# T5-bias attention and a squared-ReLU layer on one core: scores of two key tiles in one run over four banks, last queries and keys as block diagonals, six-token rows, weights in blocks

## The chip, the cores and the metric

The kernel runs on one core of a Trainium2 chip. The metric is the device time of one execution in microseconds. Inputs and output are float32; inside the kernel the operands of the matrix products are float16.

## The reference

Eight batches of eight heads, 576 tokens, head size 64. A bias that depends on the distance of query and key alone, through a table of 32 buckets, is added to the scores; the attention's output, laid out as 4608 tokens by 512, goes through two dense layers with a squared ReLU between them.

```python
scores = scale * np.matmul(q, k.transpose(0, 1, 3, 2))      # scale = 1/8
bias = bias_table[bucket]                                   # bucket of abs(i - j), 32 of them
scores = scores + bias.transpose(2, 0, 1)[None, :, :, :]
attn = softmax(scores)
x = np.matmul(attn, v)  -> (4608, 512)
h = np.maximum(x @ w_in, 0.0)                               # w_in 512 x 2048
return h * h @ w_out                                        # w_out 2048 x 512
```

## The kernel before

The work is cut into 32 head pairs (four in each batch) and nine groups of 512 tokens for the dense layers.

**A head pair** (`pair`, L492). The q and k of two heads lie in a staging tile with 128 tokens on the partitions. Five transposes on PE for each of q and k (L504) turn them into `qt` and `kt`: 128 partitions, of which 64 belong to each head, by 576 tokens. The copy out of PSUM (`copy_to`, L478) goes to ACT or DVE. Scores are computed transposed, keys on the partitions. For each of the four full key tiles (`jt` 0 to 3) and each half of the queries (288) there is one step of two matmuls (L528): each uses 64 of the 128 rows of the array, one head each, and each writes a PSUM bank of its own. The 64 tokens that are left over as keys (`jt` 4) are done by four matmuls on quarters of the array (L535). ACT takes the exponential of each step's 2 x 288 columns (L554). DVE multiplies the stretches near the diagonal by the exponentials of the bias (L574); farther off the bias is constant and drops out. PV (L612 and L619) is done for three and then two query tiles: nine matmuls for each tile, which also give the sums of the softmax; DVE divides (L636, L641). After four pairs the batch's output `x` is transposed on PE (L663) and copied to `xt`.

**A group of the dense layers** (`layers`, L693): 16 pieces of the first layer, four matmuls of 512 columns each (L758), ReLU on ACT (L778) and the square on DVE (L786); then 16 pieces of the second layer, four matmuls each (L707), a scaled copy (L727, L733) and a store.

**PSUM** has eight banks: two sets of two for scores (`st`), one for PV (`pv`), three (`f`) for transposes and the dense layers.

**What sets the order.** Nothing is issued in the order of the code. `Plan` collects every step with its engine, a guess of its cost, what it depends on, what buffers it takes and a due time. `schedule` (L88) then runs a list schedule on these guesses and the instructions are emitted in the order of their planned starts. On the chip each engine runs its list in that order and waits where it must. When PE changes between modes (`"r"` for the matmuls on 64 rows, `"q"` for the quarters, `"f"` for all others) the plan adds `SWITCH`, 60 ns. The due time of pair `p` is `nominal(p)`.

**Loads.** All of q, k, v and the weights go through POOL's queue (L243), which casts them to float16. In batch 0 q and k come by head pair: two DMAs of 128 tokens by 4 by 64 and one of 64 tokens for each (L372); in later batches by token tile, all heads at once (L395). The weights `w_in` come in four blocks of 128 rows (L436), and the first matmul of the first layer needs all four; the second layer needs all of `w_out` and all 16 squares. The bias table is built on the chip at the start and goes through DRAM once (`tdram`, L293).

Of the kernel before, what the change touches and what calls it, by code (L numbers as in the profile page):

```python
# [27 lines left out]
XR = 2560  # L28
# [43 lines left out]
LAT = {"PE": 200.0, "ACT": 90.0, "DVE": 90.0, "POOL": 120.0, "DMA": 0.0, "SP": 0.0}  # L72
SWITCH = 60.0


class Plan:
# [11 lines left out]
    def schedule(self):  # L88
        engines = ("PE", "ACT", "DVE", "POOL", "SP", "DMA")
# [57 lines left out]
    @staticmethod  # L147
    def _buf_time(op):
        t = 0.0
        for b in op.bufs:  # L150
            if b.slot is None:
                if not b.ring.free:
                    return float("inf")
                t = max(t, min(b.ring.free)[0])
        return t
# [15 lines left out]
def kernel(  # L171
# [37 lines left out]
    tr_sb = sb("tr_sb", [128, H, 384])  # L209
    tv_sb = sb("tv_sb", [H, 512])  # L210
    oh_sb = sb("oh_sb", [32, 512])
    NSTG, NQK, NPT, NV, NX, NGB, NRT, NY = 2, 5, 2, 3, 2, 2, 4, 3
    stg = [[sb(f"{n}s{i}", [128, 5, 512]) for n in "qk"] for i in range(NSTG)]
    qts = [sb(f"qt{i}", [128, S]) for i in range(NQK)]
    kts = [sb(f"kt{i}", [128, S]) for i in range(NQK)]
# [5 lines left out]
    xs = [sb(f"x{i}", [128, 5, 512]) for i in range(NX)]  # L221
    xt_sb = sb("xt", [128, 4, XR])
    gs = [sb(f"g{i}", [128, 16, GT]) for i in range(NGB)]
    rts = [sb(f"rt{i}", [128, GT]) for i in range(NRT)]
# [14 lines left out]
    def loader(eng_name, eng, out_, in_, packets, deps=(), bufs=(), due=0.0):  # L239

        issue = P.add(
            {eng_name: 800.0 if eng_name == "POOL" else 60.0},
            lambda: io(eng.dma_start(out=out_(), in_=in_())),  # L243
            deps,
            bufs,
            due,
        )
        return P.add({"DMA": packets * 27.0 / 16}, None, [issue], bufs, due), issue
# [4 lines left out]
    def load(eng_name, eng, out_, in_, packets, deps=(), bufs=(), due=0.0):  # L253
# [12 lines left out]
    l_bt = load("SP", nc.sync, const(bt_sb), const(bias_table), 32, due=0)  # L266
    l_far = load(
        "SP", nc.sync, const(far_sb), const(bias_table[NBK - 1 : NBK, :].to_broadcast([NBK, H])), 32, due=1
    )
    l_oh = load("SP", nc.sync, const(oh_sb), const(oh_d.ap()), 32, due=2)  # L270
    l_id = load("SP", nc.sync, const(id_sb), const(id_d.ap()), 128, due=3)
# [21 lines left out]
    o = load("SP", nc.sync, lambda: tdram.ap(), const(tv_sb), 64, [o])  # L293
    o = P.add({"SP": 2000.0}, None, [o])
# [6 lines left out]
            256,  # L301
# [31 lines left out]
    first = []  # L333
    for i in range(NSTG):
        for w in range(2):
            first.append(
                P.add({"DVE": 320.0}, lambda i=i, w=w: io(nc.vector.memset(stg[i][w][64:128, 4, :].bitcast(FP32), 0.0)), due=10 + i)
            )
    for i in range(NPT):
        first.append(P.add({"DVE": 90.0}, lambda i=i: io(nc.vector.memset(pts[i][:, PW:], 1.0)), due=20))  # L340
        first.append(P.add({"DVE": 90.0}, lambda i=i: io(nc.vector.memset(p4s[i][:, S:], 1.0)), due=20))
# [30 lines left out]
    def load_pair(b, w, hp):  # L372
        src = (q, k)[w]
        t = lambda: stg[b_stg[b].slot][w]
        ls = []
        for h in (2 * hp, 2 * hp + 1):
            ls.append(
                load(
                    "POOL", nc.gpsimd,
                    lambda h=h: t()[:, 0:4, ts(h, D)],  # L380
                    const(src[b, h, 0:512, :].rearrange("(t p) d -> p t d", p=128)),
                    512, first[0:4], [b_stg[b]], pdue(),
                )
            )
        ls.append(
            load(
                "POOL", nc.gpsimd,
                lambda: t()[0:64, 4, ds(128 * hp, 128)].rearrange("p (h d) -> p h d", d=D),
                const(src[b, 2 * hp : 2 * hp + 2, 512:576, :].transpose([1, 0, 2])),
                128, first[0:4], [b_stg[b]], pdue(),  # L390
            )
        )
        l_qk[b, w, hp] = ls

    def load_qk(b, w):  # L395
        src = (q, k)[w]
        t = lambda: stg[b_stg[b].slot][w]
        ls = []
        for tt in range(5):
            n = 128 if tt < 4 else 64  # L400
            ls.append(
                load(
                    "POOL", nc.gpsimd,
                    lambda tt=tt, n=n: t()[0:n, tt, :].rearrange("p (h d) -> p h d", d=D),
                    const(src[b, :, ds(128 * tt, n), :].transpose([1, 0, 2])),
                    8 * n, first[0:4], [b_stg[b]], pdue(),
                )
            )
        for hp in range(4):
            l_qk[b, w, hp] = ls  # L410

    def load_v(b):
        ls = []
        for tt in range(4):
            ls.append(
                load(
                    "POOL", nc.gpsimd,
                    lambda tt=tt: vas[b_v[b].slot][:, tt, :, 0:64],
                    const(v[b, :, ts(tt, 128), :].transpose([1, 0, 2])),
                    1024, v_fix[0] + v_fix[1] + v_fix[2], [b_v[b]], pdue(),  # L420
                )
            )
        for e in range(2):
            ls.append(
                load(
                    "POOL", nc.gpsimd,
                    lambda e=e: v4s[b_v[b].slot][ds(64 * e, 64), :, e, 0:64],
                    const(v[b, e::2, 512:576, :].transpose([1, 0, 2])),
                    256, v_fix[0] + v_fix[1] + v_fix[2], [b_v[b]], pdue(),
                )  # L430
            )
        l_v[b] = ls

    l_win, l_wout = [], []

    def load_w_in(kk):  # L436
        l_win.append(
            load("POOL", nc.gpsimd, const(w_in_sb[:, kk, :]), const(moe_w_in[ts(kk, 128), :]), 800, (), (), pdue())
        )

    def load_w_out(u):
# [5 lines left out]
                900, (), (), pdue(),  # L447
# [3 lines left out]
    for hp in range(4):  # L451
        for w in range(2):
            load_pair(0, w, hp)
        if hp == 1:
            load_v(0)
    for w in range(2):
        load_qk(1, w)
    for kk in range(4):
        load_w_in(kk)
    load_v(1)  # L460
    for u in range(4):
# [8 lines left out]
    PERIOD, LEAD, FAST = 10300.0, 12000.0, 5900.0  # L470

    def nominal(p):
        return LEAD + FAST * min(p, 5) + PERIOD * max(p - 5, 0)

    xt_ready = {}
    x_bufs = {}
# [15 lines left out]
    def pair(p):  # L492
        b, hp = divmod(p, 4)
        T = nominal(p)
        after = max(0.0, T - 9000.0)
        qb = Buf(r_qk)
        evac = []
        for w, dst in ((0, qts), (1, kts)):
            bank = Buf(r_g)

            def tr(w=w, bank=bank):
                ps = g_ps[bank.slot].bitcast(FP16)
                for t in range(5):
                    io(nc.tensor.transpose(ps[:, ts(t, 128)], stg[b_stg[b].slot][w][:, t, ts(hp, 128)], id_sb))  # L504

            o = P.add({"PE": 5 * mm(128)}, tr, l_qk[b, w, hp] + [l_id], [bank, b_stg[b]], T - 3000, after, "f")
            evac.append(
                copy_to(
                    S,
                    lambda dst=dst: dst[qb.slot],  # L510
                    lambda bank=bank: g_ps[bank.slot].bitcast(FP16)[:, 0:S],
                    [o], [bank, qb], T - 3000,
                )
            )
        pb = Buf(r_pt)
        exps = {}
        for jt in (4, 0, 1, 2, 3):
            for half in range(2) if jt < 4 else (0,):
                st = Buf(r_set)

                def score(jt=jt, half=half, st=st):
                    kt, qt, ps = kts[qb.slot], qts[qb.slot], sets_ps[st.slot]
                    for hh in range(2) if jt == 4 else (half,):
                        for e in range(2):
                            rows = ds(64 * e, 64)
                            if jt < 4:
                                io(
                                    nc.tensor.matmul(  # L528
                                        ps[:, e, 0:HQ], kt[rows, ts(jt, 128)], qt[rows, ts(hh, HQ)],
                                        start=True, stop=True,  # L530
                                    )
                                )
                            else:
                                io(
                                    nc.tensor.matmul(  # L535
                                        ps[rows, hh, 0:HQ], kt[rows, 512:576], qt[rows, ts(hh, HQ)],
                                        start=True, stop=True,
                                    )
                                )

                o = P.add(
                    {"PE": mm(HQ) + 10 if jt < 4 else 2 * mm(HQ) + 10},
                    score, evac, [st, qb], T, after, "r" if jt < 4 else "q",
                )

                def ex(jt=jt, half=half, st=st):
                    if jt < 4:
# [297 lines left out]
```

## Time and profile before

| | |
|---|---|
| median of three runs | 442.41 us (440.94 to 442.55) |
| the profiled execution's own time | 443.17 us |
| its span, from the first to the last instruction | 441.4 us |
| granted clock, mean over the span | 0.996 |
| ACT busy | 288.0 us (65%) |
| DVE busy | 210.2 us (48%) |
| POOL busy | 119.5 us (27%), all of it issuing loads |

Times in the profile are in us from the start of the span, durations of single instructions in ns. PE is the matrix engine and PEld its weight loads. Matmuls are pipelined: a matmul's duration is longer than the step from its start to the start of the next, so the steps between starts show what it costs. A group's row gives count, busy time, mean duration and, behind the second bar, the idle time ahead of it with what ended it.

### The profile page before, as it was taken

To read this page: it belongs to the slowest core of one execution; us is meant where nothing else is said; L and a number is where in the kernel's file an instruction comes from. 1 tells how busy PE (TensorE), PEld (TensorE's weight loads), DVE (VectorE), ACT (ScalarE), POOL (GpSimd) and SP (SyncE) were. 2 spreads that over 40 slices of the span, in tenths; PEclk is the share of its full clock that TensorE was granted. 3 is DMA by queue.
4 is the path that set the end of the run, shared out by engine and by line. 5 is a ranking of instruction groups with operands and counts; after the bars stand their busy time and mean duration, and the time that the engine had idled before them with its cause. 6 is when DMAs were issued, how large, how long until landed. Compare 5 with 4: busy or idle time off the path is not lost.

```text
span 441.4 us, 9092 instructions
## 1 busy us (share of the span) xinstructions
PE 417.2 (95%) x3713; PEld 209.7 (48%) x3713; DVE 210.2 (48%) x513; ACT 288.0 (65%) x495; POOL 119.5 (27%) x154
## 2 busy tenths in 40 slices
PE   1687999999999999999999999999999999999996
PEld 0265545554455445544454445544454454544442
DVE  3545556445555655455455446465544553352210
ACT  1657787667866876777767666685777766464421
POOL 7998569422162205230254007000000000000000
PEclk9998999999999999999999999999999999999999
DMA  9999999918091808980099009400010001000111
GB/s 131 159 87 165 190 166 122 137 29 76 2 133 28 74 1 74 108 55 24 26 133 79 1 25 113 68 1 25 25 50 1 25 24 49 25 25 25 48 49 72
DMA packets 122170, 29.24 MB, mean 66 GB/s; under 512 B 113896, under 2 KB 117008, under 8 KB 122128
## 3 DMA queue, kind: packets, MB, share of 16 engines
q0 software_dynamic: 115552, 18.36, 56.5%
q1 hardware_dynamic: 6576, 10.30, 6.7%
q8 instruction: 29, 0.48, 0.5%
q14 instruction: 13, 0.11, 0.1%
HBM read 37.55 MB, written 9.45 MB: 106 GB/s over the span
## 4 chain that ended last, share of the span: by engine, by line
PE 91%; DMA 3%; ACT 3%; DVE 2%; issue 1%; SPq 0%; ACTq 0%; DVEq 0%
PE f L707 30%; PE f L758 29%; PE st L528 11%; PE pv L619 9%; PE f L504 4%; PE pv L612 3%; PE st L535 3%; PE f L663 2%; ACT pt L554 2%; DMA tr_sb<-t_bias 1%; DMA t_bias<-tv_sb 1%; DMA oh_sb<-c_oh 1%; SPq L243 0%; DVE pt L574 0%; ACT y L727 0%
## 5 line engine op out<-in xcount | busy, mean ns | idle before, releaser
L554 ACT ACTIVATE pt<-st 128x576 f16<-128x576 f32 x256 | 157.3, 649 | 42.1 <-PE st L528 40.1
L707 PE MATMUL f<-w_out_sb,g 128*128 128x512 f16 x576 | 144.9, 380 | 0.4 <-ACT qt L483 0.3
L758 PE MATMUL f<-xt,w_in_sb 128*128 128x512 f16 x576 | 141.0, 380 | 0.9 <-DVE xt L485 0.4
L778 ACT ACTIVATE rt<-f 128x512 f16<-128x512 f32 x144 | 86.1, 598 | 57.1 <-PE f L758 53.2
L786 DVE TENSOR_TENSOR g<-rt 128x512 f16<-128x512 f16 x144 | 61.1, 425 | 100.6 <-ACT rt L778 100.4
L758 PEld LDWEIGHTS <-w_in_sb 128*128 128x128 f16 x576 | 51.0, 97 | 61.3 <-issue 3.8
L574 DVE TENSOR_TENSOR pt<-pt,tb_sb 128x512 f16<-128x512 f16 (+2 forms) x96 | 59.7, 623 | 40.7 <-ACT pt L554 37.7
L707 PEld LDWEIGHTS <-g 128*128 128x128 f16 x576 | 48.7, 98 | 60.8 <-issue 13.2
L528 PE MATMUL st<-qt,kt 64*128 64x288 f16 x512 | 66.2, 298 | 4.8 <-ACT pt L554 3.7
L243 POOL DMA_DIRECT2D qs<-in_q_dram x47 | 38.1, 834 | 101.4 <-PE f L504 98.1
L619 PE MATMUL pv<-va,pt 128*128 128x65 f16 x1280 | 57.2, 196 | 0.2 <-DVE pt L574 0.2
L619 PEld LDWEIGHTS <-pt 128*128 128x128 f16 x1280 | 52.6, 100 | 5.1 <-issue 0.7
L528 PEld LDWEIGHTS <-kt 64*128 64x128 f16 x512 | 20.2, 94 | 57.8 <-issue 52.9
L243 POOL DMA_DIRECT2D va<-in_v_dram x32 | 28.4, 916 | 43.0 <-PE pv L619 26.9
L243 POOL DMA_DIRECT2D ks<-in_k_dram x47 | 38.2, 858 | 6.3 <-DMA w_out_sb<-in_moe_w_out_dram 3.5
L612 PE MATMUL pv<-vm,pm 128*128 128x130 f16 x160 | 36.1, 225 | 0.2 <-DVE x L641 0.2
L641 DVE TENSOR_TENSOR x<-pv,r 128x384 f16<-128x384 f32 x64 | 31.4, 491 | 2.2
L554 ACT ACTIVATE pm<-st 128x576 f16<-128x576 f32 x32 | 20.8, 651 | 13.0 <-PE st L535 13.0
L636 DVE RECIPROCAL r<-pv 128x6 f32<-128x6 f32 x64 | 11.9, 187 | 26.0 <-PE pv L619 25.7
L727 ACT ACTIVATE y<-f 128x512 f32<-128x512 f32 x20 | 12.0, 598 | 18.6 <-PE f L707 18.2
L504 PE MATMUL f<-id_sb,qs 128*128 128x128 f16 x160 | 15.5, 234 | 4.3 <-DMA qs<-in_q_dram 4.3
L612 PEld LDWEIGHTS <-pm 128*128 128x128 f16 x160 | 15.9, 99 | 6.5 <-issue 1.4
(37 smaller groups left out, 175.7 us busy)
## 6 DMA issues: line engine op xcount, KB each, us to landing
out_dram<-y SPq DMA_DIRECT2D x36, 256.0 KB, 2.0
va<-in_v_dram POOLq DMA_DIRECT2D x32, 128.0 KB, 5.2
qs<-in_q_dram POOLq DMA_DIRECT2D x28, 128.0 KB, 4.6
ks<-in_k_dram POOLq DMA_DIRECT2D x28, 128.0 KB, 5.1
w_in_sb<-in_moe_w_in_dram POOLq DMA_DIRECT2D x4, 512.0 KB, 7.4
w_out_sb<-in_moe_w_out_dram POOLq DMA_DIRECT2D x4, 512.0 KB, 9.5
qs<-in_q_dram POOLq DMA_DIRECT2D x15, 64.0 KB, 4.8
ks<-in_k_dram POOLq DMA_DIRECT2D x15, 64.0 KB, 4.7
```

The source lines that it names most:

```text
L243: lambda: io(eng.dma_start(out=out_(), in_=in_())),
L504: io(nc.tensor.transpose(ps[:, ts(t, 128)], stg[b_stg[b].slot][w][:, t, ts(hp, 128)], id_sb))
L528: nc.tensor.matmul(ps[:, e, 0:HQ], kt[rows, ts(jt, 128)], qt[rows, ts(hh, HQ)], start=True, stop=True,)
L554: nc.scalar.activation(out=dst, in_=sets_ps[st.slot][:, :, 0:HQ], func=EXPF, scale=SCALE)
L574: io(nc.vector.tensor_tensor(out=a, in0=a, in1=t, op=MULT))
L612: nc.tensor.matmul(ps[:, i, :, :], pm[:, c : c + 128], vm[:, hp, :, 0:65], start=True, stop=False)
L619: nc.tensor.matmul(ps[:, i, e, :], pt[:, (2 * jt + e) * S + c : (2 * jt + e) * S + c + 128], va[:, jt, 2 * hp + e, 0:65], start=False, sto ...
L641: nc.vector.tensor_tensor(out=xs[xb.slot][:, qt0 : qt0 + nq, ts(hp, 128)].rearrange("p t (e d) -> p t e d", e=2), in0=ps[:, :, :, 0:64], i ...
L707: nc.tensor.matmul(g_ps[bank.slot], gs[gb.slot][:, nt, ts(m, 128)], w_out_sb[:, nt, :], start=(nt == 0), stop=(nt == 15),)
L758: nc.tensor.matmul(g_ps[bank.slot], w_in_sb[:, kk, ts(nt, 128)], xt_sb[:, kk, c : c + GT], start=(kk == 0), stop=(kk == 3),)
L778: nc.scalar.activation(out=rts[rb.slot], in_=g_ps[bank.slot], func=RELUF)
L786: nc.vector.tensor_tensor(out=gs[gb1.slot][:, nt, :], in0=rts[rb.slot], in1=rts[rb.slot], op=MULT)
```

## The change

1. **Scores in full banks.** For each key tile and head there is now one matmul of 512 queries that fills a bank (L604), and from batch 1 on two key tiles form one step of four matmuls over both sets: `run([0, 1])`, `run([2, 3])`. In batch 0 the key tiles are done singly. One exponential covers 2 x 512 columns. A step of two key tiles needs both sets free when it starts.
2. **Last queries and last keys as block diagonals.** Four small copies in each pair (L586), on DVE or on POOL as the plan finds, spread the last 64 columns of `qt` and `kt` over two 64 by 64 blocks on the diagonal of tiles `qz` and `kz` that are otherwise zero. With them the last 64 queries of both heads take four matmuls of 128 columns on the full array (L628), and the last 64 keys two of 288 columns (L653); each of the two has one exponential.
3. **Six-token rows.** In batches 0 and 1 a partition of the staging tile holds six tokens in a row, so that q and k are read in runs of 1536 bytes (384 float32) on 96 partitions in place of runs of 256 bytes. Their transposes (L559) are twelve, of 96 rows, with 64 output columns each, the two heads side by side; the copy out of PSUM puts the tokens back in order. From batch 2 on q and k are loaded by head, and the staging tile is laid out by head pair.
4. **Weights in blocks.** `w_in` comes in four blocks of 512 columns, and a piece of the first layer waits for its own block only; a quarter of the second layer waits for its own block of `w_out` and its own four squares. The order of the loads puts q, k and v of batch 0 first.
5. **The plan.** `SWITCH` is 105 ns; DMA costs are in ns for each packet; the due times come earlier (`LEAD` 8000 for 12000, `FAST` 4500 for 5900, `PERIOD` 9500 for 10300); PV is put at 300 ns a query tile in place of 508. The ring `xt` is four batches long (2304 columns), so group 4 takes its columns in two pieces. `tr_sb` lies in a buffer of the dense layers.

The functions for a transpose by DMA (`DT_QK`, `DT_X`) are not used with the values given. The diff, cut to what the steps above speak of:

```diff
-LAT = {"PE": 200.0, "ACT": 90.0, "DVE": 90.0, "POOL": 120.0, "DMA": 0.0, "SP": 0.0}
-SWITCH = 60.0
+LAT = {"PE": 200.0, "ACT": 90.0, "DVE": 90.0, "POOL": 120.0, "DMA": 1800.0, "SP": 0.0, "XB": 2000.0}
+SWITCH = 105.0
...
+    def load_six(b, w, h0, nh):
+        src = (q, k)[w]
+        l = load(
+            "POOL", nc.gpsimd,
+            lambda: six(stg[b_stg[b].slot][w])[:, h0 : h0 + nh, :],
+            const(src[b, h0 : h0 + nh].rearrange("h (p j) d -> p h (j d)", j=6)),
+            96 * nh * 107, (), [b_stg[b]], pdue(),
+        )
...
     for hp in range(4):
         for w in range(2):
-            load_pair(0, w, hp)
+            load_six(0, w, 2 * hp, 2)
         if hp == 1:
-            load_v(0)
+            load_v_tail(0, range(4))
+            for h in range(4):
+                load_v_head(0, h)
+    for h in range(4, 8):
+        load_v_head(0, h)
+    for u in range(4):
+        load_w_in(u)
...
+                if b < SIX:
+                    for j in range(6):
+                        for e in range(2):
+                            io(
+                                nc.tensor.transpose(
+                                    ps[ds(64 * e, 64), ts(j, 96)], six(t)[:, 2 * hp + e, ts(j, D)],
+                                    id_sb[0:96, 0:96],
+                                )
+                            )
...
+                spread.append(one_of({"DVE": 130.0, "POOL": 300.0}, sp, [evac[w]] + z_fix, [qb], T - 1000))
...
+        def run(jts):
+            sets = [Buf(r_set) for _ in jts]
+
+            def score():
+                kt, qt = kts[qb.slot], qts[qb.slot]
+                for jt, st in zip(jts, sets):
+                    for e in range(2):
+                        rw = ds(64 * e, 64)
+                        io(
+                            nc.tensor.matmul(
+                                sets_ps[st.slot][:, e, :], kt[rw, ts(jt, 128)], qt[rw, 0:512],
+                                start=True, stop=True,
+                            )
+                        )
+
+            o = P.add({"PE": len(jts) * mm(512) + 10}, score, evac, sets + [qb, pb], T, after, "r")
...
+        if b < 1:
+            run([0])
+            run([1])
+            last_keys()
+            run([2])
+            run([3])
+        else:
+            run([0, 1])
+            last_keys()
+            run([2, 3])
+        last_queries()
...
-                            {"PE": 4 * mm(512)}, f2, d + squares[g - 1] + l_wout, [bank, gb], 1e6, 0.0, "f"
+                            {"PE": 4 * mm(512)}, f2, d + squares[g - 1][4 * part : 4 * part + 4] + [l_wout[part]], [bank, gb], 1e6, 0.0, "f"
...
-                    {"PE": 4 * mm(512)}, f1, xt_ready[g] + l_win, [bank], due + i * 2000, 0.0, "f"
+                    {"PE": 4 * mm(512)}, f1, xt_ready[g] + [l_win[nt // 4]], [bank], due + i * 2000, 0.0, "f"
```

How the steps stand on the engines. PE's list in the middle of the program before: one step of scores (`st`, line 528) between pieces of the first layer (line 758); `kt` is the keys of a pair, `f` a bank of the dense layers, and the numbers behind the names tell buffers apart.

```order
L758 MATMUL f0_113<-xt_98,w_in_sb_62 128x512
L528 LDWEIGHTS kt2_83
L528 MATMUL st0_110<-qt2_78,kt2_83 128x288
L528 LDWEIGHTS kt2_83
L528 MATMUL st0_110<-qt2_78,kt2_83 128x288
L758 LDWEIGHTS w_in_sb_62
L758 MATMUL f1_114<-xt_98,w_in_sb_62 128x512
```

The same place of PE's list now, in a pair of batch 1: a step of two key tiles, behind the first layer (line 897) and ahead of the transposes of batch 2 (line 566).

```order
L897 MATMUL f1_119<-xt_103,w_in_sb_62 128x512
L604 LDWEIGHTS kt1_80
L604 MATMUL st0_115<-qt1_76,kt1_80 128x512
L604 LDWEIGHTS kt1_80
L604 MATMUL st0_115<-qt1_76,kt1_80 128x512
L604 LDWEIGHTS kt1_80
L604 MATMUL st1_116<-qt1_76,kt1_80 128x512
L604 LDWEIGHTS kt1_80
L604 MATMUL st1_116<-qt1_76,kt1_80 128x512
L566 LDWEIGHTS qs0_71
```

Two pairs of matmuls on half rows now stand together and fill both sets, where one pair stood alone. Counted over PE's whole list, PE leaves the full array for part of it and comes back 182 times before and 69 times now (10 and 11 of these ahead of the first matmul of the dense layers); changes from one kind of part to another, without the full array between, number 17 and 5.

POOL's list of loads at the start, before: `qs` and `ks` are the staging tiles of q and k, `va` and `vm` those of v.

```order
L243 DMA w_in_sb<-in_moe_w_in_dram 128x2048 x2
L243 DMA qs_72<-in_q_dram 128x4x64 x2
L243 DMA qs_72<-in_q_dram 64x2x64
L243 DMA ks_73<-in_k_dram 128x4x64 x2
L243 DMA ks_73<-in_k_dram 64x2x64
```

POOL's list at the start now, up to the first loads of v.

```order
L250 DMA qs_71<-in_q_dram 96x2x384
L250 DMA ks_72<-in_k_dram 96x2x384
L250 DMA qs_71<-in_q_dram 96x2x384
L250 DMA ks_72<-in_k_dram 96x2x384
L250 DMA qs_71<-in_q_dram 96x2x384
L250 DMA vm_98<-in_v_dram 64x4x64 x2
L250 DMA va_95<-in_v_dram 128x4x64 x4
```

Two loads of `w_in` stood ahead of the first q; now the first q is the first load, and one load brings a pair's q where three did. Up to the last block of `w_out` POOL issued 54 loads and now issues 36.

POOL's list now at the loads of batch 4, with the small copies (line 586) that fell to POOL.

```order
L586 COPY qz3_86<-qt3_78 64x64 x2
L250 DMA qs0_71<-in_q_dram 64x4x64 x2
L250 DMA qs0_71<-in_q_dram 128x4x64 x8
L250 DMA ks0_72<-in_k_dram 64x4x64 x2
L250 DMA ks0_72<-in_k_dram 128x4x64 x8
L586 COPY kz0_87<-kt0_79 64x64 x2
```

POOL had only loads before. Now 35 of the 128 small copies stand in its list (the other 93 in DVE's), and some of them stand behind a block of 20 loads.

More of the change, by code (lines that the diff above doesn't have):

```diff
@@ L88, in schedule @@
     def schedule(self):
-        engines = ("PE", "ACT", "DVE", "POOL", "SP", "DMA")
+        engines = ("PE", "ACT", "DVE", "POOL", "SP", "DMA", "XB")
         now = dict.fromkeys(engines, 0.0)
@@ L412, in load_v @@
[L412 to L432, printed above, removed]
@@ L502, in tr @@
                 ps = g_ps[bank.slot].bitcast(FP16)
[L503 to L514, printed above, removed]
+                t = stg[b_stg[b].slot][w]
@@ L516, in pair @@
         exps = {}
[L517 to L547, printed above, removed]
-                        dst = pts[pb.slot][:, 0:PW].rearrange("p (j e s) -> p j e s", j=4, e=2)[
-                            :, jt, :, ts(half, HQ)
-                        ]
-                    else:
-                        dst = p4s[pb.slot][:, 0:S].rearrange("p (h s) -> p h s", h=2)
@@ new lines, in last_keys, with score, ex @@
+        def last_keys():
+            st = Buf(r_set)
+            def score():
+                for half in range(2):
+                    io(
+                        nc.tensor.matmul(
+                            sets_ps[st.slot][:, half, 0:HQ], kzs[qb.slot], qts[qb.slot][:, ts(half, HQ)],
+                            start=True, stop=True,
+                        )
+                    )
+            o = P.add({"PE": 2 * mm(HQ)}, score, evac + spread[2:4], [st, qb, pb], T, after, "f")
+            def ex():
+                io(
+                    nc.scalar.activation(
+                        out=p4s[pb.slot][:, 0:S].rearrange("p (h s) -> p h s", h=2),
+                        in_=sets_ps[st.slot][:, :, 0:HQ], func=EXPF, scale=SCALE,
+                    )
+                )
+            exps["k"] = P.add({"ACT": act(S)}, ex, [o], [st, pb], T)
```

300 lines of the change are left out of this document (207 added, 93 removed).

## The prediction

> **What bounds the kernel now.** I read the page first, then the chain of waits, the timeline of PE and of the start, the groups by form, the waits and the windows. The page's busy times, PE's row in 40 slices, and the last piece of the chain:
>
> ```profile
> PE 417.2 (95%) x3713; PEld 209.7 (48%) x3713; DVE 210.2 (48%) x513; ACT 288.0 (65%) x495; POOL 119.5 (27%) x154
> PE   1687999999999999999999999999999999999996
> 422.91 14.69 PE f L707 x68
> ```
>
> PE bounds it, and only the first four slices (44 us) show it waiting. A busy PE need not be well used, so I price its work by steps between starts: 14.69 us over 68 matmuls is 0.216 us for one of 512 columns. PE's timeline in the middle of the program gives the other steps (first column: start):
>
> ```profile
> 201.34 1.04 PE L758 MATMUL f<-xt,w_in_sb 128*128 128x512 f16 x4
> 202.30 0.30 PE L528 MATMUL st<-qt,kt 64*128 64x288 f16 x2
> 202.53 1.04 PE L758 MATMUL f<-xt,w_in_sb 128*128 128x512 f16 x4
> ...
> 205.80 0.44 PE L504 MATMUL f<-id_sb,qs 128*128 128x128 f16 x5
> 206.08 0.44 PE L504 MATMUL f<-id_sb,ks 128*128 128x128 f16 x5
> ...
> 208.90 0.22 PE L612 MATMUL pv<-vm,pm 128*128 128x130 f16 x1
> ...
> 209.20 0.22 PE L612 MATMUL pv<-vm,pm 128*128 128x130 f16 x1
> ...
> 212.04 0.42 PE L528 MATMUL st<-qt,kt 64*128 64x288 f16 x4
> 212.40 1.04 PE L707 MATMUL f<-w_out_sb,g 128*128 128x512 f16 x4
> ```
>
> A transpose takes 0.28 / 5 = 0.056 us, a query tile of PV 0.30. One pair of scores between two blocks of the first layer takes 1.19 us from block to block (201.34 to 202.53); four times 0.216 is 0.86, so the pair costs 0.33. Two pairs in a row take 0.36 to their end where one takes 0.23: a pair itself is 0.125 (288 columns, the two halves at once). The rest, **0.20 us, is the price of leaving the full array and coming back**, half on each side (202.30 is 0.10 after the fourth matmul should have ended). PE does so 182 times, with 17 changes among parts at half that.
>
> The counts, from the groups by form:
>
> ```profile
> L707 PE MATMUL f<-w_out_sb,g 128*128 128x512 f16 x576 | 144.9, 380 | 0.4 <-ACT qt L483 0.3
> L758 PE MATMUL f<-xt,w_in_sb 128*128 128x512 f16 x576 | 141.0, 380 | 0.9 <-DVE xt L485 0.4 <-DVE qt L485 0.3 <-DVE y L733 0.2
> L528 PE MATMUL st<-qt,kt 64*128 64x288 f16 x512 | 66.2, 298 | 4.8 <-ACT pt L554 3.7 <-ACT pm L554 0.4
> L535 PE MATMUL st<-qt,kt 64*64 64x288 f16 x128 | 14.4, 304 | 2.0 <-ACT kt L483 0.7 <-ACT pt L554 0.7 <-DVE kt L485 0.5
> L612 PE MATMUL pv<-vm,pm 128*128 128x130 f16 x160 | 36.1, 225 | 0.2 <-DVE x L641 0.2
> L504 PE MATMUL f<-id_sb,qs 128*128 128x128 f16 x160 | 15.5, 234 | 4.3 <-DMA qs<-in_q_dram 4.3
> L504 PE MATMUL f<-id_sb,ks 128*128 128x128 f16 x160 | 14.7, 227 | 2.1 <-DMA ks<-in_k_dram 2.1
> L663 PE MATMUL f<-id_sb,x 128*128 128x128 f16 x160 | 12.9, 219 | 0.0
> ```
>
> Dense layers 1152 x 0.216 = 248.8; PV 160 x 0.30 = 48.0; transposes 480 x 0.056 = 26.9; 320 pairs of scores x 0.125 = 40.0; 182 x 0.20 + 17 x 0.10 = 38.1. Together PE's list is worth **401.8 us** of the span of 441.4; 39.6 us are waits and ends. Most of these lie ahead of the dense layers:
>
> ```profile
> 1.24 1.25 POOL L243 DMA_DIRECT2D w_in_sb<-in_moe_w_in_dram  x2 [0.79 <-POOLq L829]
> 2.46 2.12 POOL L243 DMA_DIRECT2D qs<-in_q_dram  x3
> 10.40 0.69 PE L504 MATMUL f<-id_sb,qs 128*128 128x128 f16 x5 [4.34 <-DMA qs<-in_q_dram]
> 13.65 0.65 ACT L554 ACTIVATE pm<-st 128x576 f16<-128x576 f32 x1 [0.78 <-PE st L535]
> ...
> 42.65 2.85 ACT L554 ACTIVATE pt<-st 128x576 f16<-128x576 f32 x5 [1.16 <-PE st L528]
> ...
> 50.24 2.76 PE L758 MATMUL f<-xt,w_in_sb 128*128 128x512 f16 x12 [0.36 <-DVE xt L485]
> ```
>
> The first layer starts at 50.24. By the same prices what PE's list holds ahead of it is worth 19.1, so 31.1 us are waits there, and 8.5 come later (3.8 of them behind 422.91 + 14.69 = 437.6).
>
> **Scores (PE).** Per pair the work grows a little: before 10 x 0.125 = 1.25; now four pairs of 512 columns at 0.216 + 0.004, four matmuls of 128 at 0.056 and two of 288 at 0.122: 1.35. Over 32 pairs +3.2. The 128-column last queries and the last keys run on the full array and cost no change of mode. Going and coming falls from 182 to 69 and 17 to 5: -113 x 0.20 - 12 x 0.10 = -23.8. All of it lies on PE, the bound, so it counts in full: **-20.6**, PE's list 381.2.
>
> **Six-token transposes.** 192 matmuls of 96 columns, two side by side, in place of 80. If the two run together, 96 x 0.046 = 4.4, the same as 80 x 0.056; this is in the sum above. The nearest row for the dear end is the weight load of a quarter tile:
>
> ```profile
> L535 PEld LDWEIGHTS <-kt 64*64 64x64 f16 x128 | 4.7, 106 | 11.5 <-issue 7.9 <-ACT kt L483 0.9 <-DVE pt L574 0.8
> ```
>
> If each load stands ahead of its matmul, 192 x (106 + 42) ns = 28 us, +24, of which the half in batch 0 falls into PE's waits: 0 to +12. I take **+1.5**, near the cheap end, because the second of two pairs of scores in a row (0.125 us more) shows no weight load of its own. The Trainium skill's TensorEngine Tiling (Array Packing), Restrictions, speaks against this edit: column tiles lose the fast weight load; by TensorE: Matmul & The Clock Gate, LDWEIGHTS, 64 columns then take an estimated 53 ns, so 192 would take 10.2 us, about +3 with half of it covered. No run here shows it.
>
> **The start.** POOL's first load is now q, 1.2 us earlier, with no weights ahead of it.
>
> ```profile
> qs<-in_q_dram POOLq DMA_DIRECT2D x15, 64.0 KB, 4.8
> L554 ACT ACTIVATE pt<-st 128x576 f16<-128x576 f32 x256 | 157.3, 649 | 42.1 <-PE st L528 40.1
> L554 ACT ACTIVATE pm<-st 128x576 f16<-128x576 f32 x32 | 20.8, 651 | 13.0 <-PE st L535 13.0
> L778 ACT ACTIVATE rt<-f 128x512 f16<-128x512 f32 x144 | 86.1, 598 | 57.1 <-PE f L758 53.2 <-DVE x L641 2.3
> ```
>
> With 4.8 us to landing q is there at 6.0; the first exponential came 3.25 us after the first transpose, so it starts at about 9.5. From there ACT sets the pace: 64 columns more cost 51 ns, so 1024 columns take 598 + 512 x 0.8 = 1.01 us, and a pair 4 x 1.01 + 0.60 + 0.65 = 5.3 (before 9 x 0.65 = 5.85). Four pairs are 21, with 1.5 for copies on ACT: 32. From batch 0's last exponential (45.5) to the first layer it took 4.7, so it starts at 36.5. What stands ahead of it in PE's list is worth 17.2; 19.3 us of waits in place of 31.1: **-11.8**. Between 33 (loads land in 3 us, exponentials overlap) and 42 (the loads of pairs 2 and 3 still set the pace).
>
> **What the earlier start meets.** The loads should not stop it: 36 issues in place of 54 ahead of batch 2's. ACT may:
>
> ```profile
> 60.00:70.00 10.00, 9.90 (x98) 4.97 (x97) 6.59 (x16) 8.68 (x16) 8.46 (x11) 1.00 2.44 146
> sum 80.00, PE 60.51 PEld 33.52 DVE 41.01 ACT 50.90 POOL 64.88; mean PE 7.56 PEld 4.19 DVE 5.13 ACT 6.36 POOL 8.11
> 80.00:240.00 160.00, 159.61 (x1531) 80.34 (x1530) 84.94 (x201) 115.88 (x201) 46.16 (x57) 1.00 0.71 65
> ```
>
> ACT did 50.9 us of work up to 80. Less 0.55 for each of eight pairs, 46.5 must now go between 9.5 and 66. At the busiest slice's 87% that takes 53 us, at the later 72% (115.88 of 160) 64: 0 to +7, or all of -11.8 if PE's list mixes badly. I take **+7**, the long stretch's row.
>
> **At nothing.** The small copies are no dearer than DVE's smallest multiply:
>
> ```profile
> L574 DVE TENSOR_TENSOR pm<-pm,tm_sb 128x192 f16<-128x192 f16 x32 | 8.2, 256 | 7.0 <-ACT pm L554 5.5
> ```
>
> On DVE, busy for 48%, they go between other work, a step of scores ahead of their use; with no cover, two in each pair's path at 0.26 would be 17 us. From batch 2 on q and k take 20 issues in place of 10, at 2.12 / 3 = 0.71 us each 14 us in place of 8.5; POOL waits for staging before each block (18 us, row below), so this is covered. Earlier squares and weight blocks and the shorter `xt` remove waits that PE's rows above don't show (0.4 us at L707, 0.9 at L758).
>
> **Sum.** Span 381.2 + 19.3 + 8.5 + 1.5 + 7 = 417.5, 23.9 less than 441.4. The profiled execution took 443.17, 1.77 over its span, and the median was 0.76 below it: **418.5 us**.
>
> **Rivals.**
>
> *The lead is given back:* everything up to about 80 us stays where it was, and only PE's list is shorter. 381.2 + 39.6 + 1.5 = 422.3, with the 1.0 above **423.3**. For it: ACT and POOL were full there. Chance 0.15.
>
> *Half-column transposes run one after another:* +12 in place of +1.5, **429**. Chance 0.06.
>
> *Slower: the full sets make PE wait for ACT.* A step over both sets can start only when both have been read, where before it needed one. If each of the 56 steps of batches 1 to 7 waits for one exponential of 1.01 us, that is 56 us on PE, and 418.5 + 56 = **474**. From 24 / 56 = 0.43 us a step it eats the gain.
>
> ```profile
> PE st L528 <- ACT pt L554: 3.7, 12, 0.7
> ACT pt L554 <- PE st L528: 40.1, 60, 2.1
> ```
>
> Against it: with two sets PE waited 3.7 us in all, ACT 40.1 for PE; the list puts other work between the steps. The Trainium skill names the mechanism on the page TensorEngine Tiling (Array Packing), PSUM Bottleneck: tiling speeds up the matmul, and then the evacuation of PSUM can be what is slow. Chance 0.06.
>
> *Small copies behind loads.* POOL's blocks of ten loads took 8.46 us, and a copy behind one of the new blocks holds up its pair's last scores:
>
> ```profile
> 119.66 4.22 POOL L243 DMA_DIRECT2D qs<-in_q_dram  x5 [17.85 <-PE f L504]
> 123.84 4.24 POOL L243 DMA_DIRECT2D ks<-in_k_dram  x5
> ```
>
> Half a block, 4.2 us, once in each of six batches: +25, **444**, no change. Against it: POOL idles 18 us ahead of the block. Chance 0.05.
>
> **How the numbers follow.** Forecast 0.68. Range: below, a start at 33 (-3.5), no loss to ACT (-7) and no dearer transposes (-1.5) give 406.5; above, a start at 42 (+5.5) and 7 more from ACT or the transposes give 431; 407 to 431 also holds the first two rivals. A measurement of this kernel tells about 0.5% (2.2 us) from no change. Faster 0.68 + 0.15 + 0.06 + 0.02 of the copies = 0.91; same 0.03; slower 0.06.
>
> **What would show it.** Steps of four score matmuls that end 0.44 + 0.10 us after they start; a first layer that starts near 36; ACT's exponentials of 1024 columns at 1.0 us; PE's waits for ACT still a few us. Wrong if the first layer still starts after 45, if PE idles beyond 80 us, or if scores keep their price with 69 changes.

## The result, and the profile after

422.95 us (median of four runs, 422.67 to 423.4) against 441.77 (440.94 to 442.55): ratio 0.9575, 95% interval 0.9551 to 0.96. The forecast was 418.5 in 407 to 431. The profiled execution took 422.67 us, its span is 420.9. Of all executions named below one, of the kernel with idle matmuls on 64 rows, took 1037 us and stands in no comparison.

The page of the changed kernel: busy times, PE in 40 slices and the clock granted to PE.

```profile
PE 397.9 (95%) x3697; PEld 222.1 (53%) x3697; DVE 227.0 (54%) x609; ACT 280.1 (67%) x404; POOL 154.0 (37%) x231
...
PE   4687978899999999999999999999999999999996
...
PEclk9998996999999999999999999999999999999999
```

The last piece of its chain of waits:

```profile
402.40 14.69 PE f L844 x68
```

PE still bounds it, to the same last 68 matmuls in 14.69 us. It works from the first slice on, but slices 6 to 8 (53 to 84 us), full before, are now 7, 8 and 8 tenths, and the clock falls there. First what the change was to save: PE's timeline in the middle (first column: start).

```profile
203.16 1.02 PE L897 MATMUL f<-xt,w_in_sb 128*128 128x512 f16 x4
204.12 0.60 PE L604 MATMUL st<-qt,kt 64*128 64x512 f16 x4
204.66 0.23 PE L734 MATMUL pv<-vm,pm 128*128 128x130 f16 x1
...
207.24 0.39 PE L628 MATMUL st<-qz,kt 128*128 128x128 f16 x4
207.46 1.03 PE L844 MATMUL f<-w_out_sb,g 128*128 128x512 f16 x4
```

Four dense matmuls (4 x 0.216) end at 204.02, the scores start 0.10 later; the next work starts 0.54 after the scores, which is 0.44 + 0.10. The last queries (207.24 to 207.46) pay no change. So a step of two key tiles costs what the prediction had it cost. The groups and waits that answer to its other terms:

```profile
L615 ACT ACTIVATE pt<-st 128x1024 f16<-128x1024 f32 x128 | 126.0, 1022 | 32.1 <-PE st L604 32.1
L604 PE MATMUL st<-qt,kt 64*128 64x512 f16 x256 | 43.4, 407 | 3.6 <-ACT pt L615 1.8 <-ACT pm L663 0.9 <-ACT kt L522 0.7
L628 PE MATMUL st<-qz,kt 128*128 128x128 f16 x128 | 12.8, 224 | 3.1 <-ACT pt L615 1.8 <-POOL qz L586 1.2
L653 PE MATMUL st<-qt,kz 128*128 128x288 f16 x64 | 13.8, 299 | 2.4 <-ACT pt L615 1.3 <-ACT pm L663 1.0
```

The exponential of 1024 columns takes 1.02 us, as put. For it PE waits 3.6 us in the groups of L604 and L628; with the last keys (L653) and their exponential PE's waits for ACT are 6.8 us in these three groups. ACT waits 32.1 for PE. The start, from the timeline:

```profile
5.02 0.69 PE L559 MATMUL f<-id_sb,qs 96*64 96x96 f16 x12
7.85 1.94 ACT L615 ACTIVATE pt<-st 128x1024 f16<-128x1024 f32 x2 [0.70 <-PE st L604]
15.08 0.36 DVE L320 COPY tb_sb<-g 128x768 f16<-128x768 f16 x1 [3.44 <-DMA g<-t_bias]
17.13 0.24 PE L741 MATMUL pv<-va,pt 128*128 128x65 f16 x1 [1.16 <-DVE pt L696]
18.00 0.57 PE L741 MATMUL pv<-va,pt 128*128 128x65 f16 x7 [0.63 <-DVE pt L696]
19.59 0.60 PE L604 MATMUL st<-qt,kt 64*128 64x512 f16 x2
20.24 1.02 ACT L615 ACTIVATE pt<-st 128x1024 f16<-128x1024 f32 x1 [3.43 <-PE st L604]
24.71 0.45 PE L559 MATMUL f<-id_sb,qs 96*64 96x96 f16 x12
24.99 0.42 PE L559 MATMUL f<-id_sb,ks 96*64 96x96 f16 x12
35.18 0.59 ACT L638 ACTIVATE pt<-st 128x512 f16<-128x512 f32 x1
40.49 8.79 PE L897 MATMUL f<-xt,w_in_sb 128*128 128x512 f16 x40 [0.46 <-ACT xt L522]
```

The first exponential comes at 7.85, but the first layer at 40.49 (before 50.24). Once ACT stands idle for 3.43 us: PV of the first pair stands ahead of the next scores in PE's list; it waits for DVE, and DVE had waited 3.44 us for the bias table. The last exponential of batch 0 ends at 35.77, and from there to the first layer it takes 4.7 us.

At the start PE also works more slowly: twelve transposes take 0.69 us at 5.02 and 0.45 at 24.71. The kernel before shows the same (five take 0.69 at 10.40 and 0.44 at 205.80). The PEclk row doesn't show it, because the trace's record of the clock begins only at 23.6 us (before: at 31.5). By the prediction's prices the matmuls ahead of that are worth 6.3 us now and 6.4 before (an estimate), so this slow stretch is much the same in both.

Then the stretch in which the second layer starts:

```profile
57.00:62.00 5.00, 2.89 (x31) 1.48 (x29) 2.42 (x6) 5.00 (x9) 5.00 (x7) 0.91 1.33 86
62.00:68.00 6.00, 6.00 (x87) 4.37 (x85) 3.76 (x10) 3.77 (x6) 6.00 (x9) 0.51 1.99 126
```

```profile
58.32 0.40 PE L653 MATMUL st<-qt,kz 128*128 128x288 f16 x2 [1.00 <-ACT pm L663]
...
62.51 0.65 PE L741 MATMUL pv<-va,pt 128*128 128x65 f16 x8
...
69.25 1.05 POOL L586 COPY qz<-qt 64x64 f16<-64x64 f16 x1
70.35 0.38 PE L628 MATMUL st<-qz,kt 128*128 128x128 f16 x4 [1.24 <-POOL qz L586]
70.57 1.14 PE L844 MATMUL f<-w_out_sb,g 128*128 128x512 f16 x4
```

A windows row gives the stretch, its length, then busy time (instructions) of PE, PEld, DVE, ACT and POOL, the granted clock, the DMA share and GB/s. Between 57 and 62 PE works 2.89 us of 5; no dense layer stands there in its list to fill the gaps. Then its clock is halved (0.51; by the trace's record from 61.1 to 67.9): eight PV matmuls take 0.65 where they take 0.40 elsewhere. The second layer starts at 70.57; of a lead of 9.75 us at the first layer 1.97 is left, for the kernel before has it here:

```profile
72.54 1.04 PE L707 MATMUL f<-w_out_sb,g 128*128 128x512 f16 x4
```

The same account as in the prediction: PE's list 381.2, waits ahead of the first layer 40.5 - 17.2 = 23.3, and the rest 420.9 - 381.2 - 23.3 = 16.4. Before it was 401.8 + 31.1 + 8.5. The rest and the waits together are 39.7 after 39.6: what the start won (7.8) is lost again later (7.9), and the gain is that of PE's list.

### The profile page after: what moved, and what is told of

Its sections match the earlier page's. It is cut to its first block, busy times and chain, and to the rows that moved or that the text cites. A ratio compares the mean times of both kernels' runs of the same rounds, so it can differ in the third digit from the quotient of the medians.

```text
span 420.9 us, 9103 instructions
## 1 busy us (share of the span) xinstructions
PE 397.9 (95%) x3697; PEld 222.1 (53%) x3697; DVE 227.0 (54%) x609; ACT 280.1 (67%) x404; POOL 154.0 (37%) x231
## 4 chain that ended last, share of the span: by engine, by line
PE 81%; DMA 8%; POOL 7%; issue 2%; DVE 1%; ACT 1%; POOLq 0%; ACTq 0%; DVEq 0%
PE f L844 30%; PE f L897 27%; PE pv L741 8%; PE st L604 7%; PE f L566 3%; DMA va<-in_v_dram 3%; DMA w_out_sb<-in_moe_w_out_dram 3%; POOL va L250 2%; POOL ks L250 2%; PE pv L734 2%; DMA w_in_sb<-in_moe_w_in_dram 2%; PE f L801 2%; PE st L653 1%; PE st L628 1%; POOL qs L250 1%
## 5 line engine op out<-in xcount | busy, mean ns | idle before, releaser
L615 ACT ACTIVATE pt<-st 128x1024 f16<-128x1024 f32 x128 | 126.0, 1022 | 32.1 <-PE st L604 32.1
L897 PE MATMUL f<-xt,w_in_sb 128*128 128x512 f16 (+1 forms) x640 | 142.9, 358 | 0.6 <-ACT xt L522 0.5
L897 PEld LDWEIGHTS <-w_in_sb 128*128 128x128 f16 x640 | 59.6, 98 | 58.7 <-issue 7.8
L844 PEld LDWEIGHTS <-g 128*128 128x128 f16 x576 | 52.8, 98 | 57.9 <-issue 7.0
L250 POOL DMA_DIRECT2D qs<-in_q_dram x66 | 47.2, 752 | 42.0 <-PE f L566 31.7
L250 POOL DMA_DIRECT2D ks<-in_k_dram x66 | 47.6, 826 | 0.9 <-DMA ks<-in_k_dram 0.9
L604 PE MATMUL st<-qt,kt 64*128 64x512 f16 x256 | 43.4, 407 | 3.6 <-ACT pt L615 1.8
L586 POOL COPY qz<-qt 64x64 f16<-64x64 f16 x21 | 7.6, 361 | 88.2 <-DVE qt L524 71.3
L864 ACT ACTIVATE y<-f 128x512 f32<-128x512 f32 x26 | 15.5, 598 | 19.6 <-PE f L844 19.6
L638 ACT ACTIVATE pt<-st 128x512 f16<-128x512 f32 x32 | 19.1, 598 | 3.0 <-PE st L628 2.7
```

Source lines behind the costliest of these rows:

```text
L604: nc.tensor.matmul(sets_ps[st.slot][:, e, :], kt[rw, ts(jt, 128)], qt[rw, 0:512], start=True, stop=True,)
L615: nc.scalar.activation(out=p5(pts[pb.slot])[:, jt, :, 0:512], in_=sets_ps[st.slot], func=EXPF, scale=SCALE)
L844: nc.tensor.matmul(g_ps[bank.slot], gs[gb.slot][:, nt, ts(m, 128)], w_out_sb[:, nt, :], start=(nt == 0), stop=(nt == 15),)
L897: nc.tensor.matmul(g_ps[bank.slot][:, a:z], w_in_sb[:, kk, ts(nt, 128)], xt_sb[:, kk, c : c + z - a], start=(kk == 0), stop=(kk == 3),)
```

## The experiments

The theory: PE's list gives the gain through the changes of mode; the lead of the start is lost at 57 to 80 us because the plan believes the loads slower than they are, and holds the dense work back. Rivals: the gain is a better plan; ACT's pace eats the lead; the full sets make PE wait; the small copies stand behind loads.

**The price of a change of mode.** Both kernels add one idle matmul of the identity ahead of each of the 144 pieces of the first layer, into a bank that is then overwritten; on 128 rows, and on 64 (shown).

```diff
+                    io(
+                        nc.tensor.matmul(
+                            g_ps[bank.slot][:, 0:128], id_sb[0:64, :], id_sb[0:64, :], start=True, stop=True
+                        )
+                    )
```

> The changed kernel with one idle matmul (identity by identity, 128 columns, all 128 rows of the array) put ahead of each of the 144 pieces of the first layer, into the bank that the piece then overwrites. The control of the next run. Mode-price theory: 144 x 0.056 = 8 us on PE, so 431 us; 69 changes to part of the array and back, as before. Rival (the 0.20 us belongs to the wait for a score set, not to the mode): the same, 431.

> The same idle matmul on 64 of the 128 rows. Nothing else differs from the control, but PE now leaves the full array 194 times in place of 69. Mode-price theory: 125 x 0.20 = 25 us more than the control, 456 us (454 at 0.19). Rival (the price belongs to the scores' wait): as the control, 431 within 2.

429.9 us (ratio 0.9718, 0.9686 to 0.9751) and 452.4 to 454.33 us in three executions (1.0242, 1.0213 to 1.0272). PE leaves the full array 69 times in the first and 194 in the second: (1.0242 - 0.9718) x 442.3 = 23.2 us, over 125 **0.19 us** for going and coming back. The timeline of the kernel with 64 rows:

```profile
199.83 1.04 PE L902 MATMUL f<-xt,w_in_sb 128*128 128x512 f16 x4
200.80 0.23 PE L895 MATMUL f<-id_sb 64*128 64x128 f16 x1
200.96 1.04 PE L902 MATMUL f<-xt,w_in_sb 128*128 128x512 f16 x4
```

From block to block it takes 1.13 us, 0.27 more than four dense matmuls. And the one with 128 rows:

```profile
200.08 0.22 PE L895 MATMUL f<-id_sb 128*128 128x128 f16 x1
200.14 1.03 PE L902 MATMUL f<-xt,w_in_sb 128*128 128x512 f16 x4
```

There the idle matmul costs 0.06, so half the rows cost 0.21 more for the same 128 columns. The Trainium skill's TensorEngine Tiling (Array Packing), Key Properties, says that a change of tiling mode drains TensorE; it gives no time for it, the runs do.

**Single steps.** All batches do their key tiles one at a time, as batch 0 does: 97 excursions in place of 69.

```diff
-        if b < 1:
+        if b < B:
```

> The changed kernel, but every key tile is a step of its own in all batches, as in batch 0: PE's list leaves the full array 97 times in place of 69, the matmuls are the same. By the price of a change of mode, 28 x 0.19 = +5.3 us: 428. If steps over both sets cost PE waits for ACT (the rival on the slower side), single steps are as fast as or faster than the changed kernel: 423 or less.

425.6 us (0.962, 0.9576 to 0.9663), 2.7 above the changed kernel where 5.3 was expected. The two intervals overlap (0.9551 to 0.96 there), so this run shows no saving by single steps, which speaks against the slower rival, but it doesn't show their cost. What refutes that rival is PE's waits for ACT above, 3.6 to 6.8 us in all. The clock differs too; windows of this kernel:

```profile
65.00:70.00 5.00, 3.81 (x73) 2.50 (x69) 4.81 (x13) 4.32 (x7) 4.96 (x8) 1.00 1.97 125
70.00:75.00 5.00, 3.52 (x41) 1.96 (x40) 2.66 (x7) 4.38 (x6) 4.96 (x10) 1.00 1.31 84
```

The full clock stands here (1.00) where the changed kernel has 0.71 (its row stands below, under the plan's price of loads) and 0.66; from 60 to 65 us this kernel has 0.66, the changed one 0.61.

**A better plan alone.** The kernel before with `SWITCH` 105, PV at 300 and the earlier due times.

```diff
-SWITCH = 60.0
+SWITCH = 105.0
```

> The kernel before with the changed kernel's numbers for the plan alone: 105 for a change of mode, 300 for a query tile of PV, the earlier due times. PE still leaves the full array 182 times (23 changes among parts in place of 17). Mode-price theory: PE's list is worth the same, the loads come as before, so 442 within 4 us. Rival (the gain comes from a better planned order): most of the 19 us, below 430.

440.86 us (0.9962, 0.9942 to 0.9983). It leaves the full array 182 times as before. The gain isn't that of these numbers of the plan; the prices of the loads, which the change also altered, stay here as they were before.

**The plan's price of loads.** The changed kernel; first only the four loads of `w_out` are priced lower in the plan, then all loads. No other line is changed.

```diff
# w_out
-                512 * 140, (), (), pdue(),
+                512 * 20, (), (), pdue(),
# all loads
-        return P.add({"DMA": packets / 16}, None, [issue], bufs, due), issue
+        return P.add({"DMA": 0.65 * packets / 16}, None, [issue], bufs, due), issue
```

> Only the plan's price of the four loads of w_out is changed, 20 for 140 ns a packet; the program's work and loads stay. Plan theory: PE's holes between 57 and 80 us are the plan's own, because it believes that w_out lands at 67 to 80 us where the last packet came at 50; with the price low the second layer comes earlier in PE's list and fills some of them: 3 to 5 us faster, 418 to 420. Rival (the prediction's: ACT's pace sets that stretch): within 1.5 us of 423.

> The plan's price of every load times 0.65, about what the loads took in the changed kernel's trace (the last packet of w_out at 50 us, by the plan at 80). Plan theory: the second layer starts before 62 us, PE's holes between 57 and 80 us close, 6 to 12 us faster: 411 to 417. Rival (ACT's pace): within 2 us of 423. If the loads in truth come later than this price says, PE waits for them: slower than 423.

418.18 us (0.9454, 0.9429 to 0.9478) and 407.98 (0.9223, 0.9203 to 0.9243): -4.8 and -15.0. The second layer starts at 66.74 and 59.72 in place of 70.57, the first at 40.80 and 38.19. The price of `w_out` alone gives a third of the 15.0; which other loads give the rest isn't separated. Windows of the run with all loads at 0.65:

```profile
50.00:60.00 10.00, 10.00 (x139) 6.08 (x138) 8.29 (x23) 9.39 (x15) 8.61 (x13) 1.00 1.40 92
60.00:65.00 5.00, 5.00 (x47) 2.71 (x46) 3.04 (x9) 2.23 (x4) 5.00 (x8) 1.00 1.55 98
65.00:70.00 5.00, 5.00 (x41) 2.50 (x39) 4.63 (x12) 3.48 (x5) 5.00 (x7) 1.00 1.84 160
```

The same in the changed kernel:

```profile
50.00:60.00 10.00, 8.44 (x68) 4.00 (x67) 6.95 (x20) 8.73 (x15) 9.71 (x14) 1.00 1.39 90
60.00:65.00 5.00, 4.35 (x67) 3.13 (x68) 2.87 (x6) 4.21 (x5) 5.00 (x7) 0.61 1.71 109
65.00:70.00 5.00, 3.42 (x46) 2.17 (x43) 3.85 (x12) 3.56 (x5) 4.96 (x7) 0.71 1.99 126
```

With another order alone PE has no gap, the clock stays at 1.00, and ACT does more work between 50 and 60 (9.39 of 10 in place of 8.73). ACT's pace was not the limit. The loads were in time for this order: the trace of this run shows no matmul of the dense layers waiting for a load. The chain of the changed kernel has the last of `w_out` landed at 50.01 already:

```profile
37.43 12.58 DMA w_out_sb<-in_moe_w_out_dram
```

**The small copies.** All of them on DVE; then the same with all loads at 0.65 and a copy priced at 250.

```diff
-                spread.append(one_of({"DVE": 130.0, "POOL": 300.0}, sp, [evac[w]] + z_fix, [qb], T - 1000))
+                spread.append(one_of({"DVE": 130.0}, sp, [evac[w]] + z_fix, [qb], T - 1000))
```

> The changed kernel with all 128 small copies on DVE; POOL has loads alone again. Theory: they cost nothing but the one wait of 1.2 us at 70 us, 422 to 423.5. Rival (copies behind POOL's blocks of loads hold PE up): 3 us or more faster, below 420.

> The run with all loads priced at 0.65, and the small copies on DVE alone, priced there at 250 ns as measured. Theory: as that run within 1.5 us, 407 to 409, since neither the copies nor ACT hold PE up. Rival (POOL's copies cost something once the holes are closed): 405 or less.

419.24 us (0.9486, 0.945 to 0.9523): 3.7 us below the changed kernel, where little or nothing was expected and the rival had put it below 420. 407.31 (0.9199, 0.9178 to 0.922) with the new prices, which the intervals don't tell from the prices alone; no kernel of the study was faster. Windows of the first:

```profile
60.00:65.00 5.00, 4.12 (x97) 2.89 (x91) 4.20 (x10) 5.00 (x8) 5.00 (x7) 1.00 1.60 102
65.00:70.00 5.00, 3.26 (x41) 2.07 (x42) 4.34 (x12) 3.08 (x5) 5.00 (x8) 1.00 1.92 122
```

No matmul waits for a copy on POOL any more, and the clock stays at 1.00: from 60 to 65 PE does 97 matmuls in 4.12 us, where the changed kernel does 67 in 4.35. How much of the 3.7 us is the copy's wait and how much the clock, the two profiles can't say. The clock is hardly the whole: one execution of this kernel had a mean clock of 0.991 and took 418.34 us, one of the changed kernel had 0.992 and took 423.22. Those are single executions.

**The start: row length or order.** Four runs. The first loads q and k of batches 0 and 1 by tensor, in 256-byte rows.

```diff
-    SIX = 2
+    SIX = 0
...
-            load_six(0, w, 2 * hp, 2)
+    for w in range(2):
+        load_qk(0, w)
```

> The changed kernel without the six-token rows: q and k of batches 0 and 1 are loaded by head in runs of 256 bytes and transposed by tiles of 128 tokens, as from batch 2 on; all of batch 0's q and k come ahead of its v. Theory (the earlier start comes from the loads): the first layer starts at 50 us or later in place of 40.5, 10 to 20 us slower than the changed kernel, 433 to 443, PE's list as short as ever. Rival (the rows gain nothing, the order of the loads does): within 3 us of 423.

435.23 us (0.9831), first transposes at 22.26, first layer at 57.77. This tells nothing of the rows alone: k of pair 0 stands behind ten loads of q, and since these loads wait for memsets of the staging tiles, the list put all of `w_in` ahead of them. The second loads by pair; the third does too, with `w_in` kept behind v and loads that wait for no memset; in the fourth the rows are long, and two blocks of `w_in` go first.

```diff
# by pair, 256 bytes
-            load_six(0, w, 2 * hp, 2)
+            load_pair(0, w, hp)
# the same, w_in behind v
-                512 * 140, (), (), pdue(),
+                512 * 140, (v_issue,), (), pdue(),
# long rows, w_in first
+    for u in range(2):
+        load_w_in(u)
     for hp in range(4):
```

> The changed kernel, but q and k of batch 0 are loaded by head pair in runs of 256 bytes (three loads for a pair's q or k, as the kernel before had them), in the changed kernel's order of loads and with the weights behind q, k and v; batch 1 keeps its six-token rows. If the long rows are what moves the start: 24 loads at about 0.7 us of issue in place of 8, so the first layer starts 4 to 10 us after the 40.5 of the changed kernel, at 45 to 50, and the time is 427 to 433. If the order of the loads (no weights ahead of q) does it and the row length does not: a first layer before 43 and no more than 425.

> As the run with loads by pair in 256-byte rows, which let all of w_in slip ahead of the first q (first transposes at 21.0, first layer at 54.0, 436.13 us); here those loads wait for no memset and w_in waits for the last load of v of batch 0, so the order of the loads is the changed kernel's and only the length of the rows and the number of loads differ (24 for q and k of batch 0 in place of 8). If the long rows matter by themselves: first transposes still near 5.5, but the last pair's k is issued 11 us later (16 more issues at 0.7 us), so the first layer starts 3 to 8 us after 40.5 and the time is 426 to 431. If only the weights ahead of q matter: a first layer at 40 to 42 and 422 to 424.5.

> The changed kernel with its six-token rows, but two of the four blocks of w_in stand ahead of the first q, as two did in the kernel before. If the order matters by itself: 1 MB ahead of q at the 190 GB/s of the start's rows is 5.5 us, so first transposes near 10.4, the first layer at 45 to 46 and the time 427 to 429. If the start has slack for it: first layer before 42 and 424.5 or less.

| | first transposes | first layer | time |
|---|---|---|---|
| changed kernel (long rows, q first) | 5.02 | 40.49 | 422.95 |
| 256 bytes, q first | 5.20 | 42.76 | 431.18 (0.978, 0.9747 to 0.9812) |
| long rows, two blocks of `w_in` first | 10.29 | 46.80 | 435.47 (0.9874, 0.9848 to 0.99) |
| 256 bytes, all of `w_in` first | 21.03 | 53.98 | 436.13 (0.986, 0.9825 to 0.9895) |

The second was again mixed, as `w_in` slipped ahead, and missed what was expected (427 to 433, or 425 and less). The third and fourth part the two: by the first layer, the order is worth 6.3 us and the long rows 2.3, less than the 3 to 8 expected of them. Row length and the number of loads (24 in place of 8 for q and k of batch 0) change together here and aren't parted. The times moved by more, 12.5 and 8.2, and the fourth run's expectation (427 to 429) missed. The reason stands in its timeline:

```profile
54.45 7.21 POOL L250 DMA_DIRECT2D ks<-in_k_dram  x10
...
62.77 3.66 POOL L250 DMA_DIRECT2D va<-in_v_dram  x4
...
67.72 0.23 POOL L588 COPY kz<-kt 64x64 f16<-64x64 f16 x1
68.01 0.66 PE L655 MATMUL st<-qt,kz 128*128 128x288 f16 x2 [13.04 <-POOL kz L588]
```

One small copy of 0.23 us stands in POOL's list behind ten loads of k and eight of v, and PE stands for 13.04 us. In the third run it is once 3.95 us. So the rival with the copies behind loads is a mechanism of this kernel; in the changed kernel's profile it came to a single wait of 1.24 us.

## Why the prediction was right or wrong

- **Scores, -20.6:** held. The steps cost 0.44 + 0.10, the price of a change is 0.19 (0.20 put; with 0.19 the gain of PE's list is 19.4), and what lies outside PE's list is the same in sum before and after, so the gain is that of PE's list. That the two sums are the same is luck: a gain of 7.8 and a loss of 7.9 cancel.
- **Six-token transposes, +1.5 (0 to +12):** the cheap end. At the full clock twelve take 0.28 us (24.71 to 24.99), 23 ns each; the two heads run together and the weight loads don't show. The estimate of about +3 that the prediction worked out from the Trainium skill's TensorE: Matmul & The Clock Gate, LDWEIGHTS, isn't borne out here. Cost 0.
- **The start, -11.8:** the sign held, the size was off: -7.8, a first layer at 40.5 in place of 36.5, inside the bounds 33 to 42. The step that failed is ACT's pace from the first exponential to the last of batch 0. The first came at 7.85, earlier than the 9.5 put, but the last ended at 35.77 in place of 32: the order of PE's list (PV ahead of the next scores, 3.43 us) left ACT idle at 20 us, and shorter waits for PE followed. From the last exponential to the first layer it took 4.7, as put.
- **What the earlier start meets, +7:** the size held (7.9, with the rest at 16.4 for 8.5), but by luck, for the step failed. The reason given was ACT ("ACT may") with its load up to 80 us; the run with other prices of loads has the same work on ACT, and of its span of 406.0 about 25 us lie outside PE's list of 381, in place of 39.7. What set the stretch was the planned order: no dense layer in PE's list from 57 to 70 us, and then the half clock. The price that holds the dense work back stands in the code that the diff adds (140 ns a packet for weights); I read it and didn't ask what order it makes of PE's list between 50 and 80 us.
- **"The loads should not stop it":** this held; the first layer waits 0.46 us, and that for `xt`. But POOL, busy with them from 50 to 80 us, holds the small copies.
- **At nothing, the small copies:** off. In the changed kernel's profile PE waits 1.24 us for one; with the copies on DVE the time is 3.7 us shorter; in two runs with another start PE waits 3.95 and 13.04. The chance of 0.05 for the rival was low: it goes by where the plan's guesses put a copy, not by POOL's idle time.
- **The rivals:** "the lead is given back" named 423.3, and as an account it is what happened; its reason (ACT and POOL full) holds only in POOL's part. The slower one, PE waiting for ACT on full sets, needed 24 us to eat the gain and got 3.6 on L604 and L628 (6.8 with the last keys).

In numbers: +4.0 from the start, -1.5 from the transposes, +0.9 from the later loss and +1.0 from the step from the profiled span to the median lead from 418.5 to 422.95.

## What to carry to other kernels

Count changes of mode and price them from the steps between starts: that sum carried the result here. A gain ahead of the bound's steady state only counts if the order behind it can use it; where a planner's guesses set that order, look in the new order for what fills the engine at the time the lead arrives, and try the guess of a resource's price by itself, which here was worth 15 us beside the edit's 19. Keep short work that an engine on the path waits for out of a list that also issues blocks of loads.

## What the runs showed of the hardware

- The clock can fall without a long gap. Between 57 and 62 us no wait of PE that the trace shows is over 1.00 us, it is busy for 2.89 of 5, and over 62 to 68 it gets 0.51. The Trainium skill's TensorE: Matmul & The Clock Gate, HAM oscillation, has as its rule that idle gaps of PE stay under about 3.4 us; in this trace the clock fell behind shorter ones in a row.
- Whether this stretch runs at half clock hangs on little. With the copies on DVE PE has the same waits 0.56 us earlier (1.00 us ahead of 57.76, row below, in place of 58.32; then 0.27 and 0.25 us in both), and the clock stays at 1.00 where the changed kernel has 0.61 and 0.71 (60 to 70 us). Why, these traces don't show, nor what the half clock costs: the changed kernel took 423.22 us at a mean clock of 0.992, and 422.67 to 423.4 at 0.982 to 0.984.

```profile
57.76 0.41 PE L653 MATMUL st<-qt,kz 128*128 128x288 f16 x2 [1.00 <-ACT pm L663]
```

- The PEclk row stands at full where the trace has no record of the clock. In the changed kernel the record begins at 23.6 us; ahead of it twelve transposes take 0.69 us, behind it 0.45.
- A 64 by 64 copy took 0.25 to 0.27 us in the mean on DVE and 0.36 to 0.42 on POOL; on POOL single ones took 0.23 and 1.05.

```profile
L586 DVE COPY kz<-kt 64x64 f16<-64x64 f16 x50 | 12.3, 247 | 1.8 <-ACT kt L522 0.9
L586 POOL COPY kz<-kt 64x64 f16<-64x64 f16 x14 | 5.9, 423 | 26.4 <-DVE kt L524 20.0 <-ACT kt L522 6.0
```
